# An ordering rule that emits dense matmuls as soon as their hold ends, in a two-layer attention and MLP kernel

## Chip, cores and metric

The kernel runs on one core of a Trainium2 chip. The metric is the time of one execution on the device in microseconds (us); the times shown are those of several executions of the same program.

## What is computed

Two identical layers, each an attention block and an MLP block with residuals, on x of 2048 x 512 in float32. The attention has 32 query heads of 16 and a single head of keys and values (so all heads share them); there is no mask.

```python
def _A_ref(x, wq, wk, wv, wo):            # H = 32 heads, Dh = 16
    q = (x @ wq).reshape(B, S, H, Dh).transpose(0, 2, 1, 3)
    k = x @ wk
    v = x @ wv
    p = softmax(einsum("bhqd,bkd->bhqk", q, k) * Dh ** -0.5)
    o = einsum("bhqk,bkd->bhqd", p, v)
    return o.transpose(0, 2, 1, 3).reshape(B, S, H * Dh) @ wo
def _B_ref(x, w1, w2):                    # 512 -> 1792 -> 512
    return maximum(x @ w1, 0) @ w2

x = x + _A_ref(layernorm(x)); x = x + _B_ref(layernorm(x))
x = x + _A_ref(layernorm(x)); x = x + _B_ref(layernorm(x))
```

## The kernel before

**Attention.** The 32 heads and 2048 query rows of a layer are cut into 32 units: four heads by 512 rows. A unit goes through 16 key tiles of 128 keys, so a layer has 512 steps and the kernel 1024 (`order`). A step has three kinds of work:

- two scores (`scores`, matmuls at L709): each multiplies a key tile with the queries of two heads, two matmuls on 64 rows of the array each, side by side, into one of two PSUM tiles (`st0`, `st1`) of 128 x 1024. ScalarE then takes the exponential of that tile (L710) into SBUF. The next score for the same PSUM tile has to wait until that exponential has read it.
- one product (`values`, L715): the four heads' exponentials times the values and a column of ones, into one accumulator. The products of a unit add up; after its last step VectorE copies the accumulator out (`keep`, L722). The exponentials of three steps can be held at once (three buffers), so a product may lag by up to three steps.

**Dense work.** Everything else on TensorE is written as Python generators, each of which emits a few instructions and then yields their size in units of one matmul pair or one matmul: projections of queries and keys, and for every block of 512 rows a `chain` with the output projection, the layer norm with its transposes (L275), the MLP's first half (`up`) and second half (`down`). A chain is some 390 to 466 units long. While attention runs, dense matmuls go in pairs (`batch`, L119): two jobs, each on its half of the array's rows, in two turns of 12 units. Between the turns, VectorE makes a tiny copy out of each of the two PSUM tiles (L126, tile `seen`), and the second turn waits for these. When a generator knows that its next matmuls depend on something not yet done, it yields a tuple instead; the last number is the hold, the time in us that should pass first: 0.5 between the turns, 1.0 or 1.6 after a batch, 3.2 to 3.6 ahead of transposes.

**The planner.** TensorE has one order of instructions, and it is fixed when the program is built. `timed` (L844) decides it with a small model of time: its clock `now` moves on by 0.216 us for a score, 0.858 for a product, 0.2155 for a dense unit, and 0.126 and 0.116 for going into and out of products; an exponential takes 0.925. For each turn it works out:

- `ready`: when the PSUM tile for the next score comes free; `gap` is how far off that is. It is put at 1e9 when products lag three steps, so that a product must come.
- `made`: when the next product's exponentials are there.
- `due`: the debt of dense units. Each step adds the rest of the current generator over the steps to its deadline (`rate`), each emitted unit is taken off; it is capped at `FULL`, 14.
- `free`: when the hold of the current dense work ends.
- `work`: whether there is dense work, with a debt of at least 1, that is not held.

The rules are then tried from the top (L867 to L878). One: after a product, another one if it is made and the debt is at least `PRESSED`, so that products are strung together. Two: a score, if its tile is free now, unless dense work is at hand with a debt of `FORCED`, 12. Three: a product, if it is made and the score is 0.8 us off or more (with an exception under pressure). Four: dense work, if `work`. Five: a product, if the score is 0.6 us off or more. Six: otherwise the score, for which the clock moves on to `ready`.

Nothing of this model runs on the chip: there, each instruction waits on its semaphores for what it really needs, in the order that the planner wrote down.

The kernel has a second, slower form for inputs out of range, which does not run here; its tiles have names with x, those of the form that runs have names with f (`fst`, `fp`, `facc`, `fmisc`).

Of the kernel before, what the change touches and what calls it, by code (L numbers as in the profile page):

```python
# [32 lines left out]

SCORE, VALUE, DENSE, EXP = 0.216, 0.858, 0.2155, 0.925
TO_ACT, TO_PE, ENTER, LEAVE, COPY = 0.2, 0.22, 0.126, 0.116, 1.1
PRESSED, FORCED, FULL = 6.0, 12.0, 14.0
XS, OS, VS, WS = 1.0, 64.0, 32.0, 32.0
WLO, WHI = 2.0 ** -12, 0.125

# [5 lines left out]
class _Net:  # L45
# [798 lines left out]
    def timed(self, steps, front, back, product, after):  # L844

        n = len(steps)
        now = act = due = free = sums = 0.0
        exps, done, last = [], [], None  # L850

        def turn(kind):
            nonlocal now, last
            if (kind == "product") != (last == "product"):
                now += ENTER if kind == "product" else LEAVE
            last = kind

        while len(done) < n:
            k, j = len(exps), len(done)
            step = k // 2  # L860
            ready = exps[k - 2] + TO_PE if k > 1 else 0.0
            if k == 2 * n or (step > 2 and j <= step - 3):
                ready = 1e9
            made = max(exps[2 * j + 1] + 0.1, sums) if 2 * j + 1 < k else 1e9
            work = bool(self.gens) and due >= 1.0 and now >= free
            gap = ready - now
            if last == "product" and made <= now and due >= PRESSED:  # L867
                kind = "product"
            elif gap <= (LEAVE if last == "product" else 0.0) and not (work and due >= FORCED):
                kind = "score"  # L870
            elif made <= now + ENTER and gap >= 0.8 and not (work and due >= PRESSED and last != "product" and step - j < 2):
                kind = "product"
            elif work:
                kind = "work"
            elif made <= now + 0.2 and gap >= 0.6:
                kind = "product"
            else:
                kind = "score" if ready < 1e9 else "product"  # L878
            turn(kind)
            if kind == "score":  # L880
                now = max(now, ready) + SCORE
                if k % 2 == 0:
                    before = self.spent
                    front(step)
                    now += DENSE * (self.spent - before)
                    due = min(due + self.rate(step, due), FULL) if self.gens else 0.0
                else:
                    back(step)
                act = max(act, now + TO_ACT, done[step - 3] + TO_ACT if step > 2 else 0.0) + EXP
                exps.append(act)  # L890
            elif kind == "work":
                w = self.advance()
                now += DENSE * self.worth(w)
                due -= self.worth(w)
                if isinstance(w, tuple):
                    free = now + w[3]
            else:
                now = max(now, made if made < 1e9 else 0.0) + VALUE
                product(j)
                after(j)  # L900
                done.append(now)
                sums = now + COPY if j + 1 < n and self.first(j + 1) else 0.0
# [170 lines left out]
```

## Time and profile before

| | us |
|---|---|
| times of three executions | 2611.70, 2615.32, 2617.52 |
| their median | 2615.32 |
| the profiled execution | 2610.69 |
| its span, first to last instruction | 2608.9 |
| TensorE matmuls busy | 2418.4 (93%) |
| ScalarE busy | 1987.2 (76%) |
| VectorE busy | 726.7 (28%) |
| mean granted TensorE clock | 0.986 |

In the profile, PE is TensorE's matmuls and PEld its weight loads, DVE is VectorE, ACT ScalarE, POOL GpSimd. A row of a timeline gives the start, the length, engine, line, operation, output and inputs, and how many instructions are merged in it; in square brackets stands how long the engine was idle just before, and what ended that. A row of the waits gives the waiting engine and line, what it waited for, the total in us, the number of times and the longest. A record of a matmul lasts until its results are out, so consecutive records overlap; the distance of their starts is what each takes of TensorE. One score is two instructions, one dense unit is two instructions, one product eight.

### The profile page before, as it was taken

Reading aid. Unit: us, or ns where it says so; the run is one execution under the profiler, and the core shown is the slowest. Engines: PE = TensorE matmul, PEld = TensorE weight load, DVE = VectorE, ACT = ScalarE, POOL = GpSimd, SP = SyncE. Lnnn points to the kernel's source line nnn. Section 1 sums busy time; section 2 is a strip of 40 time slices with the busy share of each in tenths; the row PEclk is TensorE's granted clock in tenths of the full one; section 3 lists DMA queues with packets and bytes.
Section 4 is the critical chain, followed back from the end, with each engine's and each line's share of the span. In section 5 each row is a group of like instructions: output and inputs, shape, how many; then the busy total and the mean of one; then the engine's idle time right before and its main releaser. Section 6 shows DMA issues by size and latency. Waiting matters only on the chain.

```text
span 2608.9 us, 44827 instructions
## 1 busy us (share of the span) xinstructions
PE 2418.4 (93%) x18957; PEld 830.9 (32%) x18957; DVE 726.7 (28%) x1556; ACT 1987.2 (76%) x2114; POOL 211.8 (8%) x291
## 2 busy tenths in 40 slices
PE   6798899999999999999798999999999999999978
PEld 2222223333333333333243222233323333333334
DVE  4545513113231132211333132321113111221132
ACT  5598897777787888888533999888888888878830
POOL 2244420000100000000100010000000000000000
PEclk9999999999999999999898999999999999999989
DMA  2034341110221112120221121211122111211032
GB/s 86 25 119 134 125 140 49 56 34 30 81 72 49 40 36 74 45 69 24 81 69 36 49 69 48 85 56 57 40 72 65 56 40 36 73 59 56 21 110 66
DMA packets 110339, 165.12 MB, mean 63 GB/s; under 512 B 19872, under 2 KB 39600, under 8 KB 110128
## 3 DMA queue, kind: packets, MB, share of 16 engines
q1 hardware_dynamic: 110128, 162.16, 19.2%
q8 instruction: 150, 2.46, 0.4%
q14 instruction: 61, 0.50, 0.1%
HBM read 116.20 MB, written 45.88 MB: 62 GB/s over the span
## 4 chain that ended last, share of the span: by engine, by line
PE 70%; ACT 21%; DVE 3%; DMA 2%; issue 2%; POOL 1%; SPq 0%; ACTq 0%; POOLq 0%; DVEq 0%
PE facc L715 30%; ACT fp L710 20%; PE fmisc L119 17%; PE fst L709 15%; PE fmisc L98 7%; DMA flsum<-fod 0%; DVE fbst L255 0%; PE fmisc L275 0%; DVE fxtl L279 0%; POOL fbmv L259 0%; DVE fxt L508 0%; PE fmisc L343 0%; POOL fkop L299 0%; DVE fxn L264 0%; SPq L370 0%
## 5 line engine op out<-in xcount | busy, mean ns | idle before, releaser
L710 ACT ACTIVATE fp<-fst 128x1024 f32<-128x1024 f32 x2048 | 1942.3, 1030 | 402.6 <-PE fst L709 385.2
L715 PE MATMUL facc<-fp,fva 128*32 128x512 f32 x8192 | 1022.0, 603 | 3.8 <-DVE faccs L722 3.8
L709 PE MATMUL fst<-fqop,fkop 64*128 64x512 f16 x4096 | 773.2, 382 | 114.6 <-ACT fp L710 96.0
L709 PEld LDWEIGHTS <-fkop 64*128 64x128 f16 x4096 | 248.8, 93 | 896.9 <-issue 761.8
L715 PEld LDWEIGHTS facc<-fp,fva 128*32 128x32 f32 x8192 | 212.6, 108 | 414.9 <-issue 374.2
L119 PE MATMUL fmisc<-fxth,fw 64*128 64x512 f16 x1376 | 236.3, 376 | 0.3 <-DVE fseen L126 0.3
L119 PE MATMUL fmisc<-fw,fhh 64*128 64x512 f16 x1344 | 222.1, 376 | 0.5 <-DVE fseen L126 0.5
L508 DVE SCALAR_TENSOR_TENSOR fxt<-fmisc,fxt 128x512 f32<-128x512 f32 x156 | 103.2, 684 | 409.1 <-PE fmisc L119 364.1
L258 POOL TENSOR_SCALAR fbmv<-fbmv 128x1 f32<-128x1 f32 x84 | 22.2, 264 | 1895.8 <-DVE fbmv L257 1894.4
L126 DVE COPY fseen<-fmisc 1x1 f32<-1x1 f32 x238 | 25.6, 142 | 473.2 <-PE fmisc L119 473.1
L119 PEld LDWEIGHTS <-fw 64*128 64x128 f16 x2064 | 106.4, 94 | 103.2 <-issue 8.3
L119 PE MATMUL fmisc<-fxtl,fw 64*128 64x512 f16 x688 | 132.6, 376 | 0.0
L119 PE MATMUL fmisc<-fw,fhl 64*128 64x512 f16 x672 | 129.0, 376 | 0.0
L722 DVE COPY faccs<-facc 128x512 f32<-128x512 f32 x64 | 44.2, 691 | 297.4 <-PE facc L715 297.4
L587 DVE TENSOR_SCALAR fhh<-fmisc 128x512 f16<-128x512 f32 x84 | 57.6, 686 | 206.9 <-PE fmisc L119 206.9
L588 DVE SCALAR_TENSOR_TENSOR fhl<-fmisc,fhh 128x512 f16<-128x512 f32 x112 | 77.4, 692 | 61.7 <-ACT fhh L585 58.8
L585 ACT ACTIVATE fhh<-fmisc 128x512 f16<-128x512 f32 x28 | 16.6, 597 | 100.0 <-PE fmisc L98 96.8
L119 PEld LDWEIGHTS <-fhh 64*128 64x128 f16 x1344 | 68.7, 94 | 59.1 <-issue 3.7
L275 PE MATMUL fmisc<-fident,fxn 128*128 128x128 f32 x336 | 56.8, 307 | 30.4 <-DVE fxn L264 27.0
L98 PE MATMUL fmisc<-fw,fhh 128*128 128x512 f16 x224 | 66.6, 379 | 0.0
L98 PE MATMUL fmisc<-fxth,fw 128*128 128x512 f16 x208 | 64.9, 390 | 0.7 <-ACT fxth L91 0.7
L255 DVE BATCH_NORM_STATS2 fbst<-fxt 128x6 f32<-128x512 f32 x84 | 57.7, 687 | 9.3 <-DMA fxt<-in_A_x_dram 5.8
(132 smaller groups left out, 1285.9 us busy)
## 6 DMA issues: line engine op xcount, KB each, us to landing
fw<-fwd SPq DMA_DIRECT2D x224, 256.0 KB
fod<-faccs SPq DMA_DIRECT2D x64, 256.0 KB
fqop<-fqd SPq DMA_DIRECT2D x128, 98.0 KB
fxt<-in_A_x_dram SPq DMA_DIRECT2D x44, 256.0 KB
fqd<-fqh SPq DMA_DIRECT2D x128, 64.0 KB
foraw<-fod SPq DMA_DIRECT2D x32, 256.0 KB
frinv<-frd SPq DMA_DIRECT2D x32, 256.0 KB
fwraw<-in_B_w_dram SPq DMA_DIRECT2D x28, 256.0 KB
```

What stands on the lines that cost most here:

```text
L98: self.nc.tensor.matmul(ps, a, b, start=(i == 0), stop=(i == n - 1))
L119: mm(ps[j], a[r], b[r], start=(turn == 0 and i == 0), stop=(turn == 1 and i == n - 1), skip_group_check=True)
L126: self.nc.vector.tensor_copy(self.wt("seen", [1, 1]), t[0:1, 0:1])
L255: nc.vector.bn_stats(st, xt)
L275: nc.tensor.transpose(ps[:, c * P:(c + 1) * P], xn[:, c * P:(c + 1) * P], self.ident)
L508: self.nc.vector.scalar_tensor_tensor(xt, ps, 1.0 / factor, xt, op0=MUL, op1=ADD)
L587: nc.vector.tensor_scalar(hh, ps, 0.0, None, op0=MAX)
L588: nc.vector.scalar_tensor_tensor(hl, ps, 0.0, _f(hh), op0=MAX, op1=SUB)
L709: nc.tensor.matmul(st[:, hf], self.kop[U // 32][h, kt * P:(kt + 1) * P], q[h, pr, :], start=True, stop=True)
L710: nc.scalar.activation(p[:, 2 * pr:2 * pr + 2], st, AF.Exp, scale=self.up ** -2)
L715: self.nc.tensor.matmul(acc[32 * j:32 * j + 32], self.va[U // 32][:, kt], p[:, 2 * pr + hf], start=start, stop=stop, skip_group_check=True)
L722: self.nc.vector.tensor_copy(self.sums[U], acc)
```

## The change

One new rule stands ahead of the last one. If dense work is owed (`due_now`) but held, and its hold ends more than half a dense unit before the next score can start, the planner moves its clock to the end of the hold and tries the rules again, which then find the dense work free. Before, it took the score and let it wait. Besides, two numbers are changed: `PRESSED` is 8 instead of 6, and in rule five the product goes ahead of a score that is 0.4 us off or more, where it was 0.6. The 0.8 of rule three is given a name and kept.

```diff
-PRESSED, FORCED, FULL = 6.0, 12.0, 14.0
+PRESSED, FORCED, FULL, LONG, SHORT = 8.0, 12.0, 14.0, 0.8, 0.4
...
-            work = bool(self.gens) and due >= 1.0 and now >= free
+            due_now = bool(self.gens) and due >= 1.0
+            work = due_now and now >= free
             gap = ready - now
...
-            elif made <= now + ENTER and gap >= 0.8 and not (work and due >= PRESSED and last != "product" and step - j < 2):
+            elif made <= now + ENTER and gap >= LONG and not (work and due >= PRESSED and last != "product" and step - j < 2):
                 kind = "product"
             elif work:
                 kind = "work"
-            elif made <= now + 0.2 and gap >= 0.6:
+            elif made <= now + 0.2 and gap >= SHORT:
                 kind = "product"
+            elif due_now and free < ready - 0.5 * DENSE and ready < 1e9:
+                now = free
+                continue
             else:
                 kind = "score" if ready < 1e9 else "product"
             turn(kind)
```

## The prediction

> **What bounds the kernel now.** I read the page first (busy time, chain, costliest groups), then the table of waits, the busy time by stretches, and last TensorE's and ScalarE's timelines.
>
> ```profile
> PE 2418.4 (93%) x18957; PEld 830.9 (32%) x18957; DVE 726.7 (28%) x1556; ACT 1987.2 (76%) x2114; POOL 211.8 (8%) x291
> PE 70%; ACT 21%; DVE 3%; DMA 2%; issue 2%; POOL 1%; SPq 0%; ACTq 0%; POOLq 0%; DVEq 0%
> L710 ACT ACTIVATE fp<-fst 128x1024 f32<-128x1024 f32 x2048 | 1942.3, 1030 | 402.6 <-PE fst L709 385.2
> ```
>
> TensorE carries the chain; ScalarE's exponentials stand idle for 402.6 us, nearly all of it waiting for scores from TensorE (L709). So time freed on TensorE counts, if it lies where TensorE is the later of the two. The stretches differ:
>
> ```profile
> core 0: us, PE busy (x) PEld busy (x) DVE busy (x) ACT busy (x) POOL busy (x), PEclk, DMA share, GB/s
> 455.00:520.00 65.00, 59.00 (x512) 22.45 (x510) 11.30 (x28) 49.49 (x53) 0.00 (x0) 1.00 0.18 56
> 1495.00:1560.00 65.00, 61.66 (x492) 17.59 (x484) 17.82 (x38) 60.26 (x64) 5.20 (x10) 1.00 0.24 75
> 1755.00:1820.00 65.00, 62.82 (x538) 21.79 (x532) 12.80 (x29) 54.68 (x59) 0.00 (x0) 1.00 0.17 56
> ```
>
> At 455 and 1755 us ScalarE has 15 and 10 us of 65 free; at 1495 us it is all but full. By the whole table, 390 to 1300 us and 1690 to 2500 us are of the first kind (dense work beside attention), 130 to 390 and 1430 to 1690 us of the second. Near 1300 to 1430 and after 2500 us dense work runs nearly alone; the change does not reach it.
>
> What the edit aims at is one row of the waits:
>
> ```profile
> PE fst L709 <- ACT fp L710: 96.0, 200, 1.0
> ```
>
> 200 times TensorE stood before a score matmul until an exponential gave its bank back, 96.0 us in all. One such wait in its surroundings:
>
> ```profile
> 437.64 0.39 PE L709 MATMUL fst<-fqop,fkop 64*128 64x512 f16 x2
> 437.87 0.38 PE L119 MATMUL fmisc<-fxtl,fw 64*128 64x512 f16 x2
> 438.09 0.59 PE L119 MATMUL fmisc<-fxth,fw 64*128 64x512 f16 x4
> 438.52 0.38 PE L709 MATMUL fst<-fqop,fkop 64*128 64x512 f16 x2
> 438.73 0.38 PE L119 MATMUL fmisc<-fxtl,fw 64*128 64x512 f16 x2
> 438.95 0.38 PE L119 MATMUL fmisc<-fxth,fw 64*128 64x512 f16 x2
> 439.21 0.39 PE L709 MATMUL fst<-fqop,fkop 64*128 64x512 f16 x2
> 440.13 0.39 PE L709 MATMUL fst<-fqop,fkop 64*128 64x512 f16 x2 [0.52 <-ACT fp L710]
> 440.34 0.39 PE L119 MATMUL fmisc<-fxth,fw 64*128 64x512 f16 x2
> 440.56 0.39 PE L119 MATMUL fmisc<-fxtl,fw 64*128 64x512 f16 x2
> 440.77 0.61 PE L119 MATMUL fmisc<-fxth,fw 64*128 64x512 f16 x4
> 441.20 0.40 PE L709 MATMUL fst<-fqop,fkop 64*128 64x512 f16 x2
> 441.42 0.40 PE L119 MATMUL fmisc<-fxtl,fw 64*128 64x512 f16 x2
> 441.63 0.61 PE L119 MATMUL fmisc<-fxth,fw 64*128 64x512 f16 x4
> 442.06 0.40 PE L709 MATMUL fst<-fqop,fkop 64*128 64x512 f16 x2
> 442.39 2.78 PE L715 MATMUL facc<-fp,fva 128*32 128x512 f32 x24
> 445.11 0.39 PE L709 MATMUL fst<-fqop,fkop 64*128 64x512 f16 x2
> 439.36 0.21 DVE L126 COPY fseen<-fmisc 1x1 f32<-1x1 f32 x2 [4.41 <-PE fmisc L119]
> 438.14 5.61 ACT L710 ACTIVATE fp<-fst 128x1024 f32<-128x1024 f32 x6 [1.85 <-PE fst L709]
> ```
>
> Read it so. Starts lie 0.2155 us apart for a pair of matmuls that runs side by side (440.34, 440.56), so one dense unit (two L119 matmuls) or one score costs 0.2155 us of TensorE, though a record lasts 0.38. From 437.64 to 445.11 three steps of attention pass in 7.47 us: six scores, 12 dense units, three products in one go (24 matmuls, 442.39 to 445.11). At 438.95 the first half of a dense batch ends; its second half is held until VectorE's two tiny copies, which end at 439.57. TensorE takes a score at 439.21, is through at 439.43, and stands for 0.70 us (0.52 by the records) until 440.13, though the dense work could go on from 439.57. The six exponentials run without a break, (5.61 - 1.02) / 5 = 0.918 us apart; then ScalarE starves through the three products (1.85).
>
> **The new last branch.** The planner holds the second half for 0.5 us from its last matmul: 438.95 + 0.2155 + 0.5 = 439.67, a good tenth behind the copies' end, so its time is true here. The old rule has nothing to do at 439.43 and takes the score. The new one sees that 439.67 lies more than half a dense unit ahead of 440.13, moves its clock there and emits dense work: units at 439.67, 439.88 and, 0.03 short of the score, one at 440.10. Of the 0.70 us, 0.46 are filled. The score comes 0.19 late, which ScalarE does not feel: the exponential of this score, the fourth, can start at 438.14 + 3 x 0.918 = 440.89 at the earliest, and the first score's row (437.64) to its exponential (438.14) shows 0.50 from issue to start, so a score as late as 440.39 is in time: 0.26 of slack.
>
> How many such places? The copies stand ahead of every second half:
>
> ```profile
> L126 DVE COPY fseen<-fmisc x238: 134/145/148, 157.7 to 2483.4; 1x1 f32<-1x1 f32 x119
> 400.41 0.39 PE L709 MATMUL fst<-fqop,fkop 64*128 64x512 f16 x2 [0.52 <-ACT fp L710]
> 2401.84 0.39 PE L709 MATMUL fst<-fqop,fkop 64*128 64x512 f16 x2 [0.52 <-ACT fp L710]
> 392.95 0.39 PE L709 MATMUL fst<-fqop,fkop 64*128 64x512 f16 x2 [0.52 <-ACT fp L710]
> 2424.45 0.39 PE L709 MATMUL fst<-fqop,fkop 64*128 64x512 f16 x2 [0.15 <-ACT fp L710]
> ```
>
> There are 119 half-batch holds. Going through TensorE's timeline in the two stretches that TensorE bounds, I gave each wait of a score the last dense matmul before it and the hold that the code states (0.5 at the half, 1.0 or 1.6 after a batch, 3.2 after transposes). At a half, 40 waits (first and last: 400.41 and 2401.84) end more than half a unit after the hold; the part behind the hold sums to 17.6 us. After whole batches and transposes the hold usually outlasts the wait (a double wait, two scores in a row, as today); 21 of those (392.95 to 2424.45) are fillable, for 9.1 us. Sum 26.7 us, or 124 units of 0.2155. In the two stretches that ScalarE bounds the same reading gives 11.6 us; there I count nothing, since the exponentials set the pace, and 5.8 (half) is the most I would allow.
>
> What is a unit worth once it is out of the way? The kernel has two gaits:
>
> ```profile
> 1065.70 1.06 PE L715 MATMUL facc<-fp,fva 128*32 128x512 f32 x8
> 1066.92 0.59 PE L119 MATMUL fmisc<-fxth,fw 64*128 64x512 f16 x4
> 1067.66 1.06 PE L715 MATMUL facc<-fp,fva 128*32 128x512 f32 x8
> ```
>
> With single products a step takes 1.96 us and serves 2 units; three steps take 5.88 with 6 units, against 7.47 with 12. Units served early let the planner walk the faster gait longer: (7.47 - 5.88) / 6 = 0.265 us each. So 124 units bring between 26.7 us (their own TensorE time) and 33 us; I take the lower, since new, shorter waits appear when the work comes in another rhythm.
>
> **Dense work taken before its data is there.** TensorE takes its work in order, so a held item that is issued too early stalls the score behind it, which it did not do when the score went first. A place where the planner's hold is too short, in a stretch that ScalarE bounds:
>
> ```profile
> 213.27 0.39 PE L709 MATMUL fst<-fqop,fkop 64*128 64x512 f16 x2 [0.90 <-ACT fp L710]
> 215.73 2.11 PE L275 MATMUL fmisc<-fident,fxn 128*128 128x128 f32 x8 [2.07 <-DVE fxn L264]
> PE fmisc L275 <- DVE fxn L264: 27.0, 15, 6.0
> ```
>
> If the transposes go ahead of the score at 213.27, ScalarE loses the exponential that this score fed during the stall, 0.918 us. Past the start I find three places of this form (near 144, 213 and 1504 us): 2.8 us, taken as a cost; at the half-batch holds none, as the copies were there 0.1 us early. [...]
>
> **The two numbers.** The gap from which a ready product is preferred to a waiting score falls from 0.6 to 0.4 us. Waits of that length with a product right behind the score: 19 in the two stretches, these the first and the last:
>
> ```profile
> 735.34 0.39 PE L709 MATMUL fst<-fqop,fkop 64*128 64x512 f16 x2 [0.27 <-ACT fp L710]
> 2493.18 0.39 PE L709 MATMUL fst<-fqop,fkop 64*128 64x512 f16 x2 [0.26 <-ACT fp L710]
> ```
>
> Were all turned round, TensorE would gain at most 0.27 + 0.17 = 0.44 us each (the record of the score ahead, 0.39, is 0.17 longer than its pitch), 8 us; ScalarE would lose 0.99 (a single product, next score after 1065.70) + 0.1 - 0.44 - 0.26 of slack = 0.39 each, 7 us. I take nothing: at a wait that short the product's own exponential has mostly just ended, or not yet, so few will turn. PRESSED (6 to 8) moves the debt at which products are strung together. The debt is a running account: each step adds 3 to 4 units (the code's 414 units over 128 steps, for one), a step with a single product serves 2. So it climbs until strings set in and hovers at the threshold; shifting the threshold shifts 2 units, 0.4 us, once per block. Taken as nothing; its other end is the first rival.
>
> **Sum.** 2610.69 (the profiled execution; its span is 2608.9) - 26.7 + 2.8 = 2586.8, that is 23.9 less. This execution lay 4.6 us below the median of the runs shown, 2615.32; from that, 2591.4.
>
> **Rivals.**
> First, slower: strings of products are broken. In the two stretches 135 strings of three stand, the one at 442.39 among them. Three products in a string take 2.72 us and 0.11 to get in (from 442.06 + 0.2155 to 442.39); a single takes 0.99 and as much to get in. Three singles are 3.30, a string 2.83: each broken string costs 0.47. If the debt mostly stands between 6 and 8 when a string would start, all 135 break, +63 us, and with the gain of 24 the kernel ends at 2654; the sign turns at 24 / 0.47 = 51 broken strings, and from 62 on it is slower by a measurable amount. With half of them broken (+32 - 24) it stands at 2623. For it: at 1065.70 singles already follow each other. Against: the account above, and 455 to 520 us, where nearly every product is in a string, so the debt there holds up through many cycles.
> Second, no change: the gap moves. Filling the half-batch hold brings the whole batch's end forward, and there the hold of 1.0 or 1.6 us finds the score waiting instead; or the time saved comes out as ScalarE at its limit, as at 1495 us. Then 2611 to 2618. Against: the end-of-batch waits are in the count of today already, and ScalarE has 10 to 15 us in 65 to spare.
> Third, a small gain: copies come late because VectorE is in the middle of something (0.69 us for one of its large operations), the planner's 0.5 is short, and about half of the 26.7 is lost to stalls of TensorE. Then 2615.32 - 13.4 + 2.8 = 2605.
> That the edit does nothing would need the debt to lie under 1 unit, or the hold to have passed, at these places; at all 61 dense work followed within 3 us of the wait, and the hold was worked out for each.
>
> **How the numbers follow.** A difference of 0.2%, 5.2 us, is about what a measurement of this kernel can tell from no change. Forecast (13 to 36 us faster, from the half-batch holds of the first stretch alone to 33 us plus part of the rest): 0.6. Third rival, or a gain past 36: 0.15. Second: 0.14. First: 0.11. So faster 0.75, same 0.14, slower 0.11. The forecast's own range is 2579 to 2602; with the unknown costs (7 us either way for the product's threshold, 5.8 for the stretches that ScalarE bounds) and most of the second rival the range is 2574 to 2613.
>
> **What would show it.** Right: the row of scores waiting for exponentials falls from 96 to about 65 us, dense matmuls start within 0.1 us of the copies' end, dense waits on the copies stay under 5 us, ScalarE's idle time falls by about 24 us, and strings of three become fewer while single products grow. Wrong: as many waits at the end of batches as were filled at the halves; or strings cut by more than half with ScalarE's busy share and the time unchanged or worse; or transposes waiting for normalised rows for much over 27 us.

## The result, and the profile after

The changed kernel takes 2575.14 us (median of 4 runs, 2569.97 to 2580.33) against 2615.58 before (4 runs, 2611.70 to 2617.52): a ratio of 0.9847 with an interval of 0.9824 to 0.987, or 40 us less. The profiled execution of it is its longest, 2580.33 us (span 2578.5); against the one of before (2610.69) it gained 30.4 us.

First the page's busy times, the chain that ended last (shares of the span by engine) and the two costliest groups that matter here:

```profile
PE 2433.6 (94%) x18945; PEld 816.8 (32%) x18945; DVE 722.8 (28%) x1554; ACT 1992.6 (77%) x2114; POOL 211.9 (8%) x291
PE 77%; ACT 10%; DVE 5%; DMA 3%; issue 2%; POOL 2%; SPq 1%; ACTq 0%; POOLq 0%; DVEq 0%
L710 ACT ACTIVATE fp<-fst 128x1024 f32<-128x1024 f32 x2048 | 1947.7, 1029 | 363.6 <-PE fst L709 345.1
L709 PE MATMUL fst<-fqop,fkop 64*128 64x512 f16 x4096 | 785.2, 383 | 47.0 <-ACT fp L710 33.3
```

The share of ScalarE in the chain halves, from 21 to 10%: the chain ran through ScalarE wherever TensorE stood before a score. ScalarE itself waits 40 us less for scores (345.1 us, from 385.2). The table of waits has the row at which the change was aimed, and the busy times by stretch show where:

```profile
PE fst L709 <- ACT fp L710: 33.3, 84, 1.0
```

```profile
455.00:520.00 65.00, 63.68 (x548) 23.08 (x546) 11.00 (x26) 51.88 (x56) 0.00 (x0) 1.00 0.17 52
1495.00:1560.00 65.00, 63.57 (x497) 18.30 (x494) 21.21 (x43) 62.46 (x65) 7.86 (x13) 1.00 0.20 61
1755.00:1820.00 65.00, 64.60 (x554) 21.83 (x547) 12.82 (x31) 54.59 (x59) 0.00 (x0) 1.00 0.19 61
```

Of 96.0 us in 200 waits, 33.3 in 84 are left. From 455 to 520 us TensorE is busy for 63.7 of 65 us where it was 59.0, and it gets through 56 exponentials' worth of scores instead of 53.

One half-batch hold of the new order, on TensorE, then the copies on VectorE and the exponentials on ScalarE:

```profile
482.29 0.38 PE L709 MATMUL fst<-fqop,fkop 64*128 64x512 f16 x2
482.50 0.60 PE L119 MATMUL fmisc<-fw,fhh 64*128 64x512 f16 x4
482.94 0.38 PE L119 MATMUL fmisc<-fw,fhl 64*128 64x512 f16 x2
483.20 0.39 PE L709 MATMUL fst<-fqop,fkop 64*128 64x512 f16 x2
483.63 0.61 PE L119 MATMUL fmisc<-fw,fhh 64*128 64x512 f16 x4
484.06 0.39 PE L119 MATMUL fmisc<-fw,fhl 64*128 64x512 f16 x2
484.27 0.40 PE L709 MATMUL fst<-fqop,fkop 64*128 64x512 f16 x2
```

```profile
483.35 0.23 DVE L126 COPY fseen<-fmisc 1x1 f32<-1x1 f32 x2 [6.16 <-PE fmisc L119]
```

```profile
482.12 7.63 ACT L710 ACTIVATE fp<-fst 128x1024 f32<-128x1024 f32 x8 [1.85 <-PE fst L709]
```

The half ends with the unit at 482.94; the copies end at 483.58; dense work starts at 483.63, three units of it, and the next score at 484.27. By the old rules that score would have been next, with 0.7 us of standing in front of it. TensorE now stands 0.21 us (483.42 to 483.63) and the score is some 0.15 later than its tile allowed, by the pitch of the exponentials before (483.20 + 0.918 = 484.12). The place is one of many: of the 118 half-batch holds of the new order, 31 have dense work within 0.06 us of the copies' end, of 119 in the old order 4. ScalarE hardly notices: eight exponentials at (7.63 - 1.02) / 7 = 0.944 us each, against 0.918.

### The profile page after: what moved, and what is told of

It is laid out like the page before. It is cut to its first block, busy times and chain, and to the rows that moved or that the text cites. A ratio compares the mean times of both kernels' runs of the same rounds, so it can differ in the third digit from the quotient of the medians.

```text
span 2578.5 us, 44807 instructions
## 1 busy us (share of the span) xinstructions
PE 2433.6 (94%) x18945; PEld 816.8 (32%) x18945; DVE 722.8 (28%) x1554; ACT 1992.6 (77%) x2114; POOL 211.9 (8%) x291
## 4 chain that ended last, share of the span: by engine, by line
PE 77%; ACT 10%; DVE 5%; DMA 3%; issue 2%; POOL 2%; SPq 1%; ACTq 0%; POOLq 0%; DVEq 0%
PE facc L715 32%; PE fmisc L119 20%; PE fst L709 17%; ACT fp L710 10%; PE fmisc L98 7%; DVE fxtl L279 1%; PE fmisc L275 1%; DVE fbst L255 1%; SPq L370 1%; DMA flsum<-fod 1%; DVE fxt L508 1%; DVE fxth L93 1%; POOL fbmv L259 1%; DMA frinv<-frd 0%; DVE fxn L264 0%
## 5 line engine op out<-in xcount | busy, mean ns | idle before, releaser
L710 ACT ACTIVATE fp<-fst 128x1024 f32<-128x1024 f32 x2048 | 1947.7, 1029 | 363.6 <-PE fst L709 345.1
L715 PE MATMUL facc<-fp,fva 128*32 128x512 f32 x8192 | 1038.2, 604 | 11.9 <-DVE faccs L722 11.6
L709 PE MATMUL fst<-fqop,fkop 64*128 64x512 f16 x4096 | 785.2, 383 | 47.0 <-ACT fp L710 33.3
L709 PEld LDWEIGHTS <-fkop 64*128 64x128 f16 x4096 | 257.5, 93 | 875.9 <-issue 728.0
L715 PEld LDWEIGHTS facc<-fp,fva 128*32 128x32 f32 x8192 | 202.6, 108 | 409.5 <-issue 354.3
L119 PE MATMUL fmisc<-fxth,fw 64*128 64x512 f16 x1376 | 237.7, 376 | 2.3 <-DVE fseen L126 1.7
L119 PE MATMUL fmisc<-fw,fhh 64*128 64x512 f16 x1328 | 222.3, 376 | 3.6 <-DVE fseen L126 1.8
L119 PEld LDWEIGHTS <-fw 64*128 64x128 f16 x2064 | 104.7, 94 | 96.1 <-issue 7.2
L119 PE MATMUL fmisc<-fxtl,fw 64*128 64x512 f16 x688 | 132.3, 376 | 0.2
L119 PE MATMUL fmisc<-fw,fhl 64*128 64x512 f16 x664 | 128.5, 376 | 0.0
L119 PEld LDWEIGHTS <-fhh 64*128 64x128 f16 x1328 | 68.8, 94 | 64.4 <-issue 12.8
L275 PE MATMUL fmisc<-fident,fxn 128*128 128x128 f32 x336 | 58.3, 308 | 31.6 <-DVE fxn L264 27.9
L255 DVE BATCH_NORM_STATS2 fbst<-fxt 128x6 f32<-128x512 f32 x84 | 57.7, 687 | 17.6 <-DMA fxt<-in_A_x_dram 12.5
```

What stands on the lines that cost most here:

```text
L119: mm(ps[j], a[r], b[r], start=(turn == 0 and i == 0), stop=(turn == 1 and i == n - 1), skip_group_check=True)
L255: nc.vector.bn_stats(st, xt)
L275: nc.tensor.transpose(ps[:, c * P:(c + 1) * P], xn[:, c * P:(c + 1) * P], self.ident)
L709: nc.tensor.matmul(st[:, hf], self.kop[U // 32][h, kt * P:(kt + 1) * P], q[h, pr, :], start=True, stop=True)
L710: nc.scalar.activation(p[:, 2 * pr:2 * pr + 2], st, AF.Exp, scale=self.up ** -2)
L715: self.nc.tensor.matmul(acc[32 * j:32 * j + 32], self.va[U // 32][:, kt], p[:, 2 * pr + hf], start=start, stop=stop, skip_group_check=True)
```

## The experiments

Each is compared with the kernel before on the same chip, with 5 rounds.

**The parts alone.** The new rule with the old numbers (`PRESSED` 6, `SHORT` 0.6):

```diff
-PRESSED, FORCED, FULL, LONG, SHORT = 8.0, 12.0, 14.0, 0.8, 0.4
+PRESSED, FORCED, FULL, LONG, SHORT = 6.0, 12.0, 14.0, 0.8, 0.6
```

> The new last rule alone, with the two numbers as before (6 and 0.6). Theory 'gaps' (what was gained are score waits that held dense work now fills): at least 30 of the 40 us, so 2585 or less, ratio 0.988 or less, and the score waits fall from 96 to under 45 us. Theory 'numbers' (the rule brings the 24 us forecast and the rest came from the two numbers): about 2591, ratio 0.991.

2578.65 us against 2614.31, ratio 0.9852 (0.9832 to 0.9871): 36 us, as the theory of the gaps has it. The score waits fall to 45.3 us, just short of the "under 45".

Only the debt of 8, in the kernel before:

```diff
-PRESSED, FORCED, FULL = 6.0, 12.0, 14.0
+PRESSED, FORCED, FULL = 8.0, 12.0, 14.0
```

> The kernel before with only the debt for strings of products raised from 6 to 8. 'Gaps': within 5 us of before, 2610 to 2620; score waits stay above 85 us; about as many strings of products. 'Numbers': 8 us or more faster, 2607 or less. The rival of broken strings: 8 us or more slower.

2614.95 us, ratio 0.9997 (0.9985 to 1.0009): no difference that the runs can tell. Its score waits are 86.7 us, from 96.0.

Only the gap of 0.4, in the kernel before:

```diff
-            elif made <= now + 0.2 and gap >= 0.6:
+            elif made <= now + 0.2 and gap >= 0.4:
```

> The kernel before with only the gap of rule five lowered from 0.6 to 0.4 us. 'Gaps': within 5 us of before; score waits fall by at most 8 us. 'Numbers': 8 us or more faster, with the score waits down by 15 us or more.

2634.10 us, ratio 1.0072 (1.0059 to 1.0085): 20 us slower, which neither theory expected.

The new rule alone, and only for the holds between the turns of a batch:

```diff
+                    hold, free = w[3], now + w[3]
...
-            elif due_now and free < ready - 0.5 * DENSE and ready < 1e9:
+            elif due_now and hold == 0.5 and free < ready - 0.5 * DENSE and ready < 1e9:
```

> The new rule alone with the old numbers, and only for the holds of 0.5 us between the two turns of a batch, not for those after batches or before transposes. By the count of fillable gaps (17.6 of 26.7 us) two thirds of what the rule alone brings: if that is 30 us or more, 20 to 25 us here, 2590 to 2595. If the other holds bring nothing or cost (transposes taken too early), as fast as the rule alone or faster. If they bring most, 2603 or more.

2595.05 us, ratio 0.9916 (0.99 to 0.9931): 19 us by the medians, 18 to 26 by the interval. The complement, with `hold != 0.5` in that line, was run later:

> The new rule alone, but only for holds other than those between the two turns: after whole batches, before transposes, after loads. If the two kinds add up: the rule alone (2579) was 36 us, the half-batch holds alone (2595) 19, so 17 here, about 2597. If the kinds hang together (a hold filled in one place shifts the rhythm so that the others find a gap): 2604 or more. By the count of gaps in the forecast (9.1 us): 2605.

2609.96 us, ratio 0.9983 (0.9972 to 0.9995): 4 us. So the two kinds of holds do not add up: 19 and 4 alone, 36 together. The 13 us left over are more than the intervals explain (about 4, 3 and 5 us either way). The score waits of the three kernels, half-batch holds, other holds, both, go the same way:

```profile
PE fst L709 <- ACT fp L710: 64.5, 135, 1.0
```

```profile
PE fst L709 <- ACT fp L710: 85.8, 179, 1.0
```

```profile
PE fst L709 <- ACT fp L710: 45.3, 110, 1.0
```

From 96.0 us the half-batch holds take 31.5, the others 10.2, both together 50.7: there the sum comes to 41.7, so 9 us of waits fall only when both kinds are filled.

**What the gap of 0.4 costs.** In the kernel with 0.4 alone TensorE stands 7.1 us before a product near 225 us, and in the changed kernel 7.2 us near 222 us; the kernel before has no such wait. In the changed kernel, TensorE's row and VectorE's:

```profile
221.78 1.08 PE L715 MATMUL facc<-fp,fva 128*32 128x512 f32 x4 [7.21 <-DVE faccs L722]
```

```profile
217.71 0.70 DVE L255 BATCH_NORM_STATS2 fbst<-fxt 128x6 f32<-128x512 f32 x1 [9.84 <-DMA fxt<-in_A_x_dram]
```

A unit's last product has been moved behind the statistics of newly loaded rows; VectorE waits 9.84 us for that load, the copy of the accumulator stands behind it and starts at 221.04, and the next unit's first product waits for the copy. This is the theory of the queue (what stands behind a waiting operation on VectorE waits with it), and four runs were made for it. First the changed kernel with 0.6, and with the debt of 6:

```diff
-PRESSED, FORCED, FULL, LONG, SHORT = 8.0, 12.0, 14.0, 0.8, 0.4
+PRESSED, FORCED, FULL, LONG, SHORT = 8.0, 12.0, 14.0, 0.8, 0.6
```

```diff
-PRESSED, FORCED, FULL, LONG, SHORT = 8.0, 12.0, 14.0, 0.8, 0.4
+PRESSED, FORCED, FULL, LONG, SHORT = 6.0, 12.0, 14.0, 0.8, 0.4
```

> The changed kernel with the gap of rule five back at 0.6 us: new rule and debt 8. Theory 'queue' (0.4 costs because one product moves and, near 220 us, the copy of the accumulator lands on VectorE behind a statistic that waits for a load; TensorE then stands 7 us): that wait is gone, and the time is 5 us or more under the changed kernel's 2575, so 2570 or less. Theory 'additive' (each part keeps the price that it had alone: rule -36, debt 0, gap +20): about 2579. If 0.4 is worth having beside the rule: 2580 or more.

> The changed kernel with the debt back at 6: new rule and gap 0.4. 'Additive': about 2599, 20 us over the rule alone. 'Queue': what 0.4 costs hangs on whether the copy of the accumulator near 220 us stands behind the waiting statistic; with such a wait 5 to 10 us over the rule alone (2584 to 2589), without it within 5 us of it (2574 to 2584).

Rule and debt: 2575.53 us, ratio 0.9855 (0.9835 to 0.9876), the same as the changed kernel, where the theory of the queue said 2570 or less. Rule and gap: 2580.91, ratio 0.9877 (0.9859 to 0.9896), 2 us over the rule alone. So beside the new rule the 20 us are gone; the prices are not additive. The two equal times hide different waits, though: the kernel with rule and debt has no wait of 7 us near 222, but it has one of 5.66 us before transposes near 1560 us, where the changed kernel has one of 1.01. Then a longer hold after those loads, in the changed kernel and in the kernel with 0.4 alone:

```diff
-        yield ("lag", 1, 0.0, 4.0)
+        yield ("lag", 1, 0.0, 12.0)
```

> The changed kernel, all three parts, with the hold after the loads of a later block's rows put at 12 us where it was 4, so that their statistics are queued on VectorE when the loads have mostly landed. 'Queue': the 7.2 us wait of a product for the accumulator's copy near 222 us is gone and the time is 5 to 10 us under the changed kernel, 2565 to 2570. 'Additive' or a cause elsewhere: within 4 us of 2575.

> The kernel before with the gap 0.4 alone, and the same hold of 12 us after these loads. 'Queue': the 7.1 us wait near 225 us and the transposes' waits near 1606 us are gone, so 10 us or more under the 2634 that 0.4 alone gave: 2624 or less. If 0.4 costs by making scores late all along: within 5 us of 2634.

2585.32 us (ratio 0.9896, 0.9879 to 0.9914) and 2636.46 (1.0078, 1.0063 to 1.0093). The long waits for the accumulator are gone in both, and neither is faster; the first is 10 us slower than the changed kernel. But that does not settle the theory of the queue, for waits of the same kind have come up elsewhere. In the changed kernel with the longer hold, VectorE's row and TensorE's:

```profile
227.89 0.42 DVE L748 SCALAR_TENSOR_TENSOR fgood<-flsum,fgood 128x32 f32<-128x32 f32 x2 [5.21 <-DMA flsum<-fod]
```

```profile
233.88 1.12 PE L275 MATMUL fmisc<-fident,fxn 128*128 128x128 f32 x4 [6.94 <-DVE fxn L264]
```

VectorE waits 5.21 us for another load, the statistics of the rows now stand behind it, and the transposes wait 6.94 us for these rows. In the kernel with 0.4 alone and the longer hold the same happens near 1607 us: VectorE waits 8.38 us for that load, the transposes 6.82 us, where they waited 3.23 us without that hold. In all, transposes wait for normalised rows 38.1 us in the first (27.9 in the changed kernel) and 37.3 us in the second (31.1 with 0.4 alone). So the longer hold moved the waiting rather than removed it, and what the queue has to do with the 20 us stays open.

The other theory is that a product in so short a gap makes the score late. The kernel before, with 0.4 only where dense work is owed:

```diff
-            elif made <= now + 0.2 and gap >= 0.6:
+            elif made <= now + 0.2 and gap >= (0.4 if self.gens and due >= 1.0 else 0.6):
```

> The kernel before with the gap of rule five at 0.4 only where dense work is owed and held, 0.6 elsewhere. Theory 'late scores' (a product that takes a gap of 0.4 to 0.6 makes the next score 0.5 to 0.7 late, past its slack of 0.26, and ScalarE starves about 0.4 each time): most of such places are of this kind, about two thirds or more, so 2626 or more, with ScalarE's waits for scores 10 us or more over the 385 of before. Rival 'unowed' (the 20 us come from the places without owed work, where ScalarE sets the pace): within 5 us of before, 2610 to 2620.

2637.24 us, ratio 1.0085 (1.0069 to 1.01): the places where dense work is owed carry the whole loss, and ScalarE waits 409.4 us for scores, 24 more than before. TensorE's rows at one of them (L119's left out), and ScalarE's:

```profile
426.04 0.39 PE L709 MATMUL fst<-fqop,fkop 64*128 64x512 f16 x2
426.36 1.92 PE L715 MATMUL facc<-fp,fva 128*32 128x512 f32 x16
428.22 0.61 PE L709 MATMUL fst<-fqop,fkop 64*128 64x512 f16 x4
429.72 0.39 PE L709 MATMUL fst<-fqop,fkop 64*128 64x512 f16 x2 [0.90 <-ACT fp L710]
430.05 1.09 PE L275 MATMUL fmisc<-fident,fxn 128*128 128x128 f32 x8
```

```profile
428.65 3.94 ACT L710 ACTIVATE fp<-fst 128x1024 f32<-128x1024 f32 x4 [1.09 <-PE fst L709]
433.68 2.85 ACT L710 ACTIVATE fp<-fst 128x1024 f32<-128x1024 f32 x3 [1.09 <-PE fst L709]
```

Products go in at 426.36 although a score is nearly due. ScalarE runs dry for 1.09 us; then two scores go in at once (428.22), both tiles are full, no product is left and the transposes are held, so TensorE stands 0.90 us. Both engines wait, one after the other, and five microseconds later (433.68) again. In the changed kernel, between the same transposes:

```profile
413.41 1.92 PE L715 MATMUL facc<-fp,fva 128*32 128x512 f32 x16
415.26 0.61 PE L709 MATMUL fst<-fqop,fkop 64*128 64x512 f16 x4
415.80 1.15 PE L275 MATMUL fmisc<-fident,fxn 128*128 128x128 f32 x8
416.88 0.39 PE L709 MATMUL fst<-fqop,fkop 64*128 64x512 f16 x2
```

The order begins alike, but the transposes go where the 0.90 us of standing was. This place shows how the new rule can fill what 0.4 opens; that it does so everywhere was not tried.

Nor is such a place where most of the time goes. This run has the wait for the accumulator too (7.1 us near 225 us). With the starts of the same score compared in the two timelines, it falls 21 us behind the kernel before after the first 64 scores of 2048: 8.0 us from score 128 to 192, where that wait stands, 5.4 us from 1152 to 1280, and only 0.8 us from 320 to 384, where the place shown stands. In the tables of waits, TensorE's waits for the accumulator grow by 7.0 us with 0.4 alone and by 9.7 in this run, those for exponentials by 9.2 and 11.8. So both theories have a share in the 20 us, and no run separates them.

**Holds that are too short.** The new rule alone, with a hold between the turns that ends before the copies:

```diff
-                yield ("lag", 0, 1.0, 0.5)
+                yield ("lag", 0, 1.0, 0.2)
```

> The new rule alone (debt 6, gap 0.6), and the planner's hold between the two turns of a batch put at 0.2 us instead of 0.5, which is before the copies can have ended (they end about 0.4 after the last matmul's slot). Theory 'gaps with true holds': dense work is emitted too early, TensorE stands before it (its waits for the copies rise from 7 us to 20 or more) and the score behind it waits too; the gain shrinks, 2584 or more against the rule alone at 2579. Rival 'any early dense work helps, TensorE's order forgives a short hold': within 4 us of 2579 or faster.

2592.70 us, ratio 0.9924 (0.9904 to 0.9945): 14 us of the 36 are lost. TensorE's wait for the copies, in the rule alone and here:

```profile
PE fmisc L119: 7.2, 17
```

```profile
PE fmisc L119: 11.6, 28
```

The direction is the expected one, the size of this row is not: 4.4 us more, where 13 or more were expected. Where the rest of the 14 us lies is not shown.

**A try at more.** The new rule, 0.6, and a debt of 10:

```diff
-PRESSED, FORCED, FULL, LONG, SHORT = 8.0, 12.0, 14.0, 0.8, 0.4
+PRESSED, FORCED, FULL, LONG, SHORT = 10.0, 12.0, 14.0, 0.8, 0.6
```

> A try at more: the new rule, gap 0.6, and the debt for strings at 10. Theory 'debt hovers at its threshold': within 5 us of the same kernel with debt 8 (2575.5). Rival 'fewer strings feed ScalarE better': 2570 or less, with ScalarE's waits for scores under 330 us and more single products. Rival 'strings save TensorE': 2581 or more.

2573.90 us, ratio 0.9852 (0.9836 to 0.9868): the same as with 8.

## Why the prediction was right, and where its sizes were off

The time went the way that was forecast, by 40 us where 24 were forecast. It lies below the forecast's own 2579 to 2602, and only 1 us inside the wider range of 2574 to 2613. That range was wide for costs that were not known (the gap of 0.4, the stretches that ScalarE bounds) and not for what made the gain larger, so that it still holds the time is in part luck.

*The fill of the half-batch holds* was right in place, way and size: 17.6 us forecast, 19 measured with these holds alone. In the two stretches that TensorE bounds, score waits whose last dense matmul before them ends a half come to 27.4 us before and to 2.4 with these holds alone.

*The fill of the other holds* was mis-sized, and this is the step that failed: 9.1 us, to be added to the first. Alone they bring 4, beside the half-batch holds 36 - 19 = 17. A count of gaps in the old order cannot see it. In the same two stretches all other score waits come to 52.8 us before; filling the other holds takes 7.4 off that alone, and 13.4 (46.7 to 33.3) when the half-batch holds are filled too. The likely reason, which no run isolates, is that batches then end at other points of the rhythm of scores, where the longer holds do find a gap. The prediction's second rival, that at the end of a batch the gap would open anew, falls: there the waits went down.

*The score waits* were to fall to about 65 us and fell to 33.3. With the new rule alone they fell to 45.3, for the same reason; the rest goes with the two numbers.

*What a unit is worth.* I had taken the lower end, the TensorE time filled. The profiles don't give this price. By the page, TensorE is idle for 144.9 us, from 190.5, and busy for 15.2 us more: 45.6 - 15.2 = 30.4 us. Score waits fell by 62.7 us, so other waits grew by 17.1, those for the accumulator's copy alone from 3.8 to 11.6 us, most of it the one wait near 222 us. The 15.2 us of busy time have two candidates, the lower clock of the profiled execution (0.980 against 0.986) and more strings of products (733 against 663, a single product counted as a string), which the prediction would price at some 16 us. The run with rule and gap, at a clock of 0.986, has 54 strings more than before and is busy for only 3.0 us more; the run with the hold of 0.2, at the same clock and with as many strings, for 14.9 more. So the number of strings doesn't set it, and the 0.47 us for a broken string is not confirmed. Strings of three went from 160 to 119 and singles from 462 to 561. The rule alone takes them to 134 and 526, as foreseen: with fewer waits the planner walks the faster gait longer.

*The debt of 8* was taken at nothing, and the intervals show nothing, alone (0.9997) or beside the rule (2575.5 with, 2578.7 without it); a gain of some 4 us is not excluded (see the end). The rival of broken strings falls: 41 strings of three fewer, and no loss. (The two stretches hold 144 such strings, not 135, so that it would have cost up to 68 us instead of 63.)

*The gap of 0.4* was taken at nothing, with 7 us either way. Alone it costs 20 us, far outside; the bound came from waits with a product right behind the score in the two stretches that TensorE bounds. It counted neither what a moved product does to VectorE's queue, as near 222 us, nor what a late score does beside held transposes. ("At most 0.44 us each" was too low as well: seven of the 19 waits are 0.365 us long in the records, not 0.27.) Beside the new rule it costs nothing that can be measured, so the total did not suffer from the error.

*Dense work too early* was priced at 2.8 us. Dense work on the copies waits 3.4 us in the changed kernel (1.4 before), transposes on normalised rows 27.9 (27.0); with the rule alone it is 7.2 and 32.2. A hold set too short does cost: with 0.2 there are 28 waits for the copies instead of 17, and 14 us are lost.

## What to carry to other kernels

A static order that can only choose "what is ready now" or "the main stream's next item" left TensorE standing before 200 scores here, 96.0 us in all; letting it wait for whatever comes free soonest took that to 45.3 us and brought 36 us of 2614. The hold in the planner has to match the chip: one of 0.2 us, where the copies end some 0.4 us after the matmul's slot, lost 14 of the 36. What a rule fills in the old order is not what it brings: 17.6 us counted and 19 measured, 9.1 and 4, but 26.7 and 36 for both together, likely since filled gaps shift the rhythm, which no run isolates. A threshold that costs nothing beside one set of rules can cost 0.7% under another, so try the parts of a change alone and beside each other. And an experiment that removes one wait has to be searched for the wait that took its place.

## What the runs showed of the hardware beyond that

Three executions with the same order of TensorE at the start lie up to 5.3 us apart within the first 107 us, at different granted clocks. The clock is the third number from the right in these rows of busy times; first the kernel before, then the changed one, then the changed one with the debt of 6, from 0 to 65 and from 65 to 130 us:

```profile
0.00:65.00 65.00, 39.14 (x190) 14.21 (x191) 31.91 (x78) 37.34 (x42) 17.99 (x37) 0.92 0.30 87
65.00:130.00 65.00, 52.39 (x320) 16.83 (x319) 33.25 (x62) 35.48 (x38) 17.74 (x22) 0.97 0.08 24
```

```profile
0.00:65.00 65.00, 39.72 (x182) 14.17 (x182) 31.21 (x77) 36.20 (x40) 17.99 (x37) 0.87 0.29 87
65.00:130.00 65.00, 52.47 (x288) 16.29 (x284) 31.20 (x59) 32.94 (x35) 16.70 (x21) 0.89 0.07 22
```

```profile
0.00:65.00 65.00, 39.18 (x192) 14.21 (x192) 31.91 (x78) 37.72 (x42) 17.98 (x37) 0.92 0.29 87
65.00:130.00 65.00, 52.02 (x319) 16.77 (x318) 33.25 (x62) 35.52 (x38) 17.75 (x22) 0.97 0.08 25
```

TensorE's order is the same in these three kernels up to some 140 us, so that it can't be what differs: the same four transposes start at 102.2 us in the first, 107.1 in the second and 101.8 in the third. The changed kernel's four runs order themselves by the mean clock: 0.986, 0.984, 0.982 and 0.980 go with 2569.97, 2574.01, 2576.27 and 2580.33 us. The profiled execution of before drew 0.986 and that of the changed kernel 0.980, which fits that the profiles differ by 30 us and the medians by 40. The rows show both pairs of clocks (0.92 and 0.97, 0.87 and 0.89) with one order at the start; from 130 to 195 us all three show 1.00. Why the clock differs from run to run and stays uneven for 130 us, no run shows.

This bears on small differences. Over all runs with a clock on record, 0.001 of mean clock goes with 1.8 us within a kernel. An estimate at equal clocks, from a straight line fitted to these runs and good to about 2 us, puts the new rule alone at 35 us, the debt of 8 at 4 us alone, 4 beside the rule and 7 beside rule and gap, and the gap of 0.4 at 15 us lost alone and within 2 us of nothing when it is added to the rule or to rule and debt. At 0.980, for one, the rule with the debt of 8 took 2581.47 us and the rule alone 2586.50.
